# Other pacing of two lonely transforms, joint turns of two gradients in one PSUM bank, and two coefficient planes in one operation

## The chip, the core and the metric

The kernel runs on one core of a Trainium2 chip. The core has TensorE (called PE in the profile: matmuls; PEld: its weight loads), VectorE (DVE), ScalarE (ACT), GpSimd (POOL) and SyncE (SP), which here issues DMA transfers. The metric is the device time of one execution in microseconds, lower is better. Before the change the median of three runs is 1794.33 us (1794.07 to 1795.59).

## What is computed

The kernel computes a forward pass and its gradients. The input is x of shape 2048 x 576 in bf16, normalized over the last axis to xn. Two branches of xn are added to x: an S4 state space convolution (128 states for each of 576 channels, a causal convolution of length 2048 done with Fourier transforms), and a gated feed-forward layer (FFN) with a ReLU gate and 4608 hidden columns. Outputs are the result and the gradients of x, of the S4 parameters and of the three FFN weights.

```python
def _A_ref(u, A_re, A_im, B_re, B_im, C_re, C_im, log_dt, Dskip):      # S4, shortened
    dt = exp(log_dt)[:, None]
    P = exp((dt * A)[:, :, None] * l)
    K = einsum("dn,dnl,dn->dl", Cc, P, dt * Bc).real                   # the convolution's kernel
    y = irfft(rfft(pad(u)) * rfft(pad(K)))[:L]
    return y + u * Dskip
def _B_ref(x, W_gate, W_up, W_down):                                   # FFN
    gate = relu(x @ W_gate); h = gate * (x @ W_up)
    return h @ W_down
out = x + _A_ref(xn, ...) + _B_ref(xn, ...)                            # and the gradients of all inputs
```

## The kernel before

Two Python generators emit the instructions. The FFN generator is the main stream and runs over 12 chunks of 384 hidden columns. The S4 generator is woven in between: each `yield` says how many units of work were just emitted, and S4 is advanced while its sum is under 0.9 (`PACE`) of the FFN's. At the string "last", just before the final pass first needs the transforms' result, whatever is left of S4 is emitted at once.

```python
for us in ffn.gen(ln, final):
    if us == "last":
        if s4_open:
            s4_open = False
            for r in sgen:
                stt += r
        continue
    ft += us
    ...
    while s4_open and stt < PACE * (ft - start):
        r = next(sgen, None)
        ...
```

S4 works on two halves of the channels. `p1` transforms the input and the output gradient and multiplies them, `p2` builds the convolution's kernel and the parameter gradients, `p3` transforms that kernel and forms the results. `p1(0)` runs beside the parameter preparation only and `p3(1)` beside nothing else of S4; these are the lonely ones, with four buffers per pool (n = 4). The others share their time with a `p2` (n = 2). `gap` is what is yielded between the first loads of a stage and its first matmul.

```python
yield from self.both(self.p1(0, 4, 10.0), 68.0, self.params(pw), 45.0)
with ExitStack() as c:
    pools = self.p2_pools(c)
    yield from self.both(self.p2(0, pools, pw), 0.8 * W2, self.p1(1, 2, 3.0), W1)
    yield from self.both(self.p2(1, pools, pw), 0.8 * W2, self.p3(0, 2, 3.0), W3)
yield from self.p3(1, 4, 8.0)
```

A transform has three stages with results passed through DRAM: forward (`fwd1`, matmuls on L628, result A), mixing (`mix`, `product`, `unmix`: L645, L655, result C) and, in `p1`, a backward step (`back2`, L686). The last stage of `p3` is done by the final pass, which loads C.

```python
def fwd1(self, hf, ns, load, ap, op, n, gap):
    ...
    for n2 in range(ST):                         # ST = 16
        ...
            if n2 == 0:
                yield gap
        ...                                      # per ri: ns matmuls, each with one eviction
            if ri == 0:
                yield 0.2 * ns
        nc.sync.dma_start(self.A[ns][hf][:, n2], A[:])
        yield 0.2 * ns

# p1, mixing: f = 1.0 if n < 4 else 1.25; per h of 16: two mix() at f * 0.3, a product at f * 0.7,
#             an unmix() at f * 0.65; p3, mixing: f = 1.0 if n < 4 else 2.0
# p1, backward: per n2 of 16 two matmuls (L686), one eviction, yield 0.5
```

In the FFN, `a_unit` computes gate, up and the gradient of h for 128 hidden columns and 512 rows, and from them T with three parts: h, and the gradients of gate and up. Parts of earlier units are turned (transposed by TensorE, L270) between its matmul groups (L244), since the weight gradients need them the other way round; `t_steps` does that, one part per step, and `g.bal.copy` (L62 on VectorE, L68 on ScalarE) takes the result out of PSUM.

```python
self.hN = wp.tile([P, ST, Fc], BF16, name="hN")
self.dgN = wp.tile([P, ST, Fc], BF16, name="dgN")
self.duN = wp.tile([P, ST, Fc], BF16, name="duN")
...
def a_unit(self, c, sg, ft, turns=()):
    src = self.t_steps(turns)
    ...
    for i, rhs in enumerate((xT, xT, gT)):
        ...
        ps = g.psum_mm.tile([P, 512], F32, name="ps_mm")
        for k in range(NK):
            nc.tensor.matmul(ps[:], lhsT=w[:, k, fs], rhs=rhs[:, k, :], start=(k == 0), stop=(k == NK - 1))
        pss.append(ps)
        for _ in turns:
            next(src)
        yield NK * 0.2158 + len(turns) * 0.22
    ...                                          # relu (L253), mask (L254), T (L256, L261)

def t_steps(self, units):
    for c, sg, ft in units:
        for src, dst in zip(self.T[(c, sg, ft)], (self.hN, self.dgN, self.duN)):
            pt = g.psum_mm.tile([P, 512], F32, name="ps_mm")[:].bitcast(BF16).rearrange(...)
            for j in range(JS):                  # JS = 4
                nc.tensor.transpose(out=pt[:, j, :], in_=src[:, j * P:(j + 1) * P], identity=g.ident_bf[:])
            g.bal.copy(dst[:, sg * JS:(sg + 1) * JS, ft * P:(ft + 1) * P], pt[:, 0:JS, :], 512, fp32=False)
            yield
```

The pool `psum_mm` has 5 banks, the S4 pool 3. The coefficients that the last part of the change touches are applied 36 times in `p2`, on VectorE (L867 to L869):

```python
v.tensor_tensor(w1, pw[:, 2, hs]..., X[:, :, 1:3, :]..., op=ALU.mult)
v.tensor_tensor(w2, pw[:, 3, hs]..., X[:, :, 0:2, :]..., op=ALU.mult)
v.tensor_tensor(XC[:]..., w1, w2, op=ALU.subtract)
```

## Time and profile before

| | before |
|---|---|
| median of 3 runs | 1794.33 us |
| span in the profile | 1792.3 us |
| TensorE busy | 1719.7 us |
| VectorE busy | 1317.8 us |
| ScalarE busy | 1189.2 us |
| moved by DMA | 373.30 MB, mean 208 GB/s |
| turned parts taken out of PSUM | 432 copies of 128 x 512 bf16; the 412 on ScalarE have a median of 580 to 592 ns, the 20 on VectorE of 420 to 424 |

The profile is a page on one execution, with views that can be asked by stretch of time, by line or by tile. In the table of stretches each row is a stretch, in microseconds from the start: its length, the busy time of PE, PEld, DVE, ACT and POOL (in brackets the number of instructions), the clock that TensorE was granted (1.00 is full), the mean busy share of the 16 DMA engines, and GB/s. The chain of waits is the work that ended last, followed back from the end: start, length and what it was; a DMA in it is a transfer that something waited for. In the list of waits each line has the engine, what waited, and what for, with the total in us, the number of times and the longest. Busy TensorE is modelled: matmuls overlap, so small gaps between them do not show as idle.

### The profile page before, as it was taken

The numbers are of one execution on the slowest core, as the hardware profiler recorded it, in microseconds if no ns is written. First come the engines' busy times: TensorE is split into PE (matmuls) and PEld (weight loads), VectorE is DVE, ScalarE is ACT, GpSimd is POOL, SyncE is SP. The second block draws the span as 40 slices with busy tenths as digits, with TensorE's granted clock in tenths as the row PEclk, the third lists the DMA queues.
The fourth block names the chain that finished last, engine by engine and source line by source line (L and its number), as shares of the span: only waits on it lengthen the run. The fifth ranks groups of instructions, "written<-read, shape, count | busy, mean of one in ns | idle before, by whom it ended". The sixth has DMA issues, their size and how long they took to land.

```text
span 1792.3 us, 42070 instructions
## 1 busy us (share of the span) xinstructions
PE 1719.7 (96%) x16449; PEld 1184.7 (66%) x16449; DVE 1317.8 (74%) x2867; ACT 1189.2 (66%) x2736; POOL 205.0 (11%) x246
## 2 busy tenths in 40 slices
PE   7989989999999999999999999999999998999998
PEld 5665557667667666766766766766676675676776
DVE  7575884677789788678787889889978962972551
ACT  5875874786688477568468658747857845864651
POOL 0200112011022011012101101101111100110000
PEclk9999999999999999999999999999999999999999
DMA  9799989679568656766858856866766578995873
GB/s 297 265 332 303 331 233 295 194 182 253 165 145 228 192 139 157 226 183 147 229 154 190 230 156 142 212 188 151 181 185 152 112 212 257 260 288 157 270 240 100
DMA packets 239004, 373.30 MB, mean 208 GB/s; under 512 B 49491, under 2 KB 153429, under 8 KB 237269
## 3 DMA queue, kind: packets, MB, share of 16 engines
q1 hardware_dynamic: 212836, 304.09, 52.4%
q0 software_dynamic: 24384, 51.92, 18.6%
q10 hardware_dynamic: 1584, 14.60, 2.3%
q8 instruction: 129, 2.11, 0.5%
q14 instruction: 71, 0.57, 0.1%
HBM read 233.10 MB, written 137.43 MB: 207 GB/s over the span
## 4 chain that ended last, share of the span: by engine, by line
PE 63%; DVE 21%; ACT 7%; DMA 6%; issue 3%; SPq 1%; POOL 0%; ACTq 0%; DVEq 0%; POOLq 0%
PE ps_mm L298 17%; PE ps_mm L244 15%; PE ps_mm L352 11%; PE ps_mm L336 6%; PE ps_mm L270 3%; DVE V L935 2%; DVE T L261 2%; DVE Sm L936 2%; DVE V L881 1%; DVE Y L882 1%; DVE Y L880 1%; DVE rg L254 1%; PE ps_mm L370 1%; DMA gT<-in_gT_dram 1%; DVE X L861 1%
## 5 line engine op out<-in xcount | busy, mean ns | idle before, releaser
L298 PE MATMUL ps_mm<-wf,T 128*128 128x288 bf16 x3456 | 481.8, 287 | 7.4 <-DVE T L256 2.6
L298 PEld LDWEIGHTS <-T 128*128 128x128 bf16 x3456 | 324.5, 98 | 97.0 <-issue 12.9
L68 ACT CAST osx<-ps_mm 128x288 bf16<-128x288 f32 x682 | 260.5, 428 | 50.5 <-PE ps_mm L298 47.6
L311 POOL DMA_DIRECT2D acc_dram<-osx x160 | 138.8, 867 | 1027.8 <-ACT osx L68 590.7
L352 PEld LDWEIGHTS <-rows 128*128 128x128 bf16 x1536 | 146.2, 98 | 95.4 <-issue 1.6
L244 PE MATMUL ps_mm<-xT,wd_150 128*128 128x512 bf16 x720 | 181.1, 379 | 4.1 <-ACT xT L153 1.6
L270 PEld LDWEIGHTS <-T 128*128 128x128 bf16 x1728 | 127.5, 98 | 86.3 <-issue 4.7
L244 PE MATMUL ps_mm<-xT,wd_151 128*128 128x512 bf16 x720 | 180.8, 380 | 0.0
L254 DVE SCALAR_TENSOR_TENSOR rg<-rg,ps_mm 128x512 bf16<-128x512 bf16 x144 | 98.2, 682 | 108.3 <-PE ps_mm L244 68.6
L244 PE MATMUL ps_mm<-gT,wd_152 128*128 128x512 bf16 x705 | 175.9, 379 | 0.7 <-DMA gT<-in_gT_dram 0.7
L270 PE MATMUL ps_mm<-ident_bf,T 128*128 128x128 bf16 x1728 | 157.6, 220 | 4.8 <-DVE T L256 1.9
L336 PE MATMUL ps_mm<-rows,hN 128*128 128x144 bf16 x2304 | 158.9, 227 | 0.0
L336 PEld LDWEIGHTS <-hN 128*128 128x128 bf16 x2304 | 148.5, 98 | 8.0 <-issue 5.4
L68 ACT CAST obw<-ps_mm 128x384 bf16<-128x384 f32 x103 | 49.2, 478 | 144.7 <-PE ps_mm L352 112.4
L352 PE MATMUL ps_mm<-dgN,rows 128*128 128x384 bf16 x768 | 136.8, 326 | 0.5 <-DMA rows<-xs_dram_141 0.5
L352 PE MATMUL ps_mm<-duN,rows 128*128 128x384 bf16 x768 | 135.6, 326 | 0.0
L253 ACT ACTIVATE rg<-ps_mm 128x512 bf16<-128x512 f32 x144 | 86.9, 603 | 52.1 <-PE ps_mm L244 51.5
L68 ACT CAST dhb<-ps_mm 128x512 bf16<-128x512 f32 x141 | 83.8, 594 | 49.6 <-PE ps_mm L244 47.7
L261 DVE TENSOR_TENSOR T<-dhb,rg 128x1024 bf16<-128x1024 bf16 x141 | 101.0, 717 | 19.4 <-ACT dhb L68 18.7
L244 PEld LDWEIGHTS <-wd_150 128*128 128x128 bf16 x720 | 66.0, 97 | 61.5 <-issue 3.7
L244 PEld LDWEIGHTS <-wd_151 128*128 128x128 bf16 x720 | 65.4, 98 | 59.9 <-issue 3.3
L244 PEld LDWEIGHTS <-wd_152 128*128 128x128 bf16 x705 | 63.4, 98 | 58.8 <-issue 1.8
(2506 smaller groups left out, 3042.2 us busy)
## 6 DMA issues: line engine op xcount, KB each, us to landing
acc_dram<-osx POOLq DMA_DIRECT2D x176, 288.0 KB, 5.1
gT<-in_gT_dram SPq DMA_DIRECT2D x48, 640.0 KB, 6.2
xT<-xT_dram SPq DMA_DIRECT2D x44, 640.0 KB, 5.8
rows<-in_gq_dram SPq DMA_DIRECT2D x48, 576.0 KB, 4.3
wf<-in_Wf_dram ACTq DMA_DIRECT2D x11, 1296.0 KB, 8.9
ex_dram<-exs SPq DMA_DIRECT2D x36, 320.0 KB, 4.6
ex<-ex_dram SPq DMA_DIRECT2D x36, 320.0 KB, 4.5
out_dram<-obw SPq DMA_DIRECT2D x96, 96.0 KB, 2.7
```

The lines of the kernel that those rows point to most:

```text
L68: self.nc.scalar.copy(out, in_)
L244: nc.tensor.matmul(ps[:], lhsT=w[:, k, fs], rhs=rhs[:, k, :], start=(k == 0), stop=(k == NK - 1))
L253: nc.scalar.activation(rg, ps_g[:], ACT.Relu)
L254: nc.vector.scalar_tensor_tensor(upm, rg, 0.0, ps_u[:], op0=ALU.is_gt, op1=ALU.mult)
L261: nc.vector.tensor_tensor(T[:, 1:3], dhb.unsqueeze(1).to_broadcast([P, 2, JS * P]), ru[:], op=ALU.mult)
L270: nc.tensor.transpose(out=pt[:, j, :], in_=src[:, j * P:(j + 1) * P], identity=g.ident_bf[:])
L298: nc.tensor.matmul(ps[:, cs], lhsT=lt, rhs=rh, start=(i == 0), stop=(i == len(mms) - 1))
L311: nc.gpsimd.dma_start(g.acc_dram[:, t, :, :], o[:], accum_op=ALU.add)
L336: nc.tensor.matmul(ps[:, ft * 144:(ft + 1) * 144], lhsT=self.hN[:, st, ft * P:(ft + 1) * P], rhs=gq[:, st, :], start=(st == 0), stop=(st = ...
L352: nc.tensor.matmul(ps[:, :Fc], lhsT=xs[:, st, 0:P], rhs=src[:, st, :], start=(st == 0), stop=(st == ST - 1))
L935: nc.vector.tensor_tensor(pr[:, vi], X[:, dx:dx + DG, r0:r0 + 2].rearrange("p d r a -> p d (r a)").unsqueeze(2).to_broadcast(sh), psg[:, 0 ...
L936: nc.vector.tensor_reduce(out=Sm[:, :, s0 + dd:s0 + dd + DG, :].rearrange("p v d j -> p v (d j)"), in_=pr.rearrange("p v d j c -> p v (d j ...
```

## The change

Four things change. The first and the last stage of the lonely transforms yield more per piece, so that they are spread over more FFN work; the mixing of `p1(0)` yields less, the gaps are shorter, and the weights of `p1(0)` against the parameter preparation change. The parameter preparation computes its coefficient rows before its exponentials. The two gradients are turned together, eight transposes into one bank and one copy out into a common tile `gN`, and the turns are dealt out anew between the three matmul groups. The two coefficient products in `p2` become one operation with a hand-built overlapping view of X, for which the two coefficient rows swap places. The purpose of the first is to keep TensorE from waiting at the turns of stages; the others save instructions with a fixed cost.

```diff
--- before.py
+++ after.py
@@ -168,8 +168,8 @@
         self.wd = [wp.tile([P, NK, Fc], BF16, name=f"wd{i}") for i in range(3)]
         self.wf = wp.tile([P, 3, FTC, D], BF16, name="wf")
         self.hN = wp.tile([P, ST, Fc], BF16, name="hN")
-        self.dgN = wp.tile([P, ST, Fc], BF16, name="dgN")
-        self.duN = wp.tile([P, ST, Fc], BF16, name="duN")
+        self.gN = wp.tile([P, 2, ST, Fc], BF16, name="gN")
+        self.dgN, self.duN = self.gN[:, 0], self.gN[:, 1]
         g.xtp = pool("ffn_xt", 2)
         self.tp = pool("ffn_t", 2 * FTC - 1)
         self.ep = pool("ffn_e", 2)
@@ -243,9 +243,10 @@
             for k in range(NK):
                 nc.tensor.matmul(ps[:], lhsT=w[:, k, fs], rhs=rhs[:, k, :], start=(k == 0), stop=(k == NK - 1))
             pss.append(ps)
-            for _ in turns:
+            n = (2 * len(turns) * (i + 1)) // 3 - (2 * len(turns) * i) // 3
+            for _ in range(n):
                 next(src)
-            yield NK * 0.2158 + len(turns) * 0.22
+            yield NK * 0.2158 + n * 0.33
         ps_g, ps_u = pss[0:2]
         shp = [P, JS * P]
         ru = self.ep.tile([P, 2, JS * P], BF16, name="rg")
@@ -264,11 +265,17 @@
     def t_steps(self, units):
         g, nc = self.g, self.g.nc
         for c, sg, ft in units:
-            for src, dst in zip(self.T[(c, sg, ft)], (self.hN, self.dgN, self.duN)):
+            src, js, fs = self.T[(c, sg, ft)], slice(sg * JS, (sg + 1) * JS), slice(ft * P, (ft + 1) * P)
+            for which in ((0,), (1, 2)):
+                n = len(which) * JS
                 pt = g.psum_mm.tile([P, 512], F32, name="ps_mm")[:].bitcast(BF16).rearrange("p (k t) -> p k t", t=P)
-                for j in range(JS):
-                    nc.tensor.transpose(out=pt[:, j, :], in_=src[:, j * P:(j + 1) * P], identity=g.ident_bf[:])
-                g.bal.copy(dst[:, sg * JS:(sg + 1) * JS, ft * P:(ft + 1) * P], pt[:, 0:JS, :], 512, fp32=False)
+                for i, w in enumerate(which):
+                    for j in range(JS):
+                        nc.tensor.transpose(out=pt[:, i * JS + j, :], in_=src[w][:, j * P:(j + 1) * P], identity=g.ident_bf[:])
+                if n == JS:
+                    g.bal.copy(self.hN[:, js, fs], pt[:, 0:n, :], n * P, fp32=False)
+                else:
+                    g.bal.copy(self.gN[:, :, js, fs], pt[:, 0:n, :].rearrange("p (i j) t -> p i j t", i=2), n * P, fp32=False)
                 yield
 
     def outdx(self, c, sg, j, last=None, turns=()):
@@ -587,9 +594,6 @@
                 nc.sync.dma_start(self.ex_dram[:, i], ex[:])
                 bal.add(d=0.75, a=0.65)
 
-            for i in range(0, 8):
-                ex_step(i)
-                yield 1.0
             p1 = pool.tile([P, D], F32, name="p1")
             p2 = pool.tile([P, D], F32, name="p2")
             v.scalar_tensor_tensor(pw[:, 1, :], Ai, 1.0 / TWO_PI, dt[:], op0=ALU.mult, op1=ALU.mult)
@@ -597,10 +601,10 @@
                 v.tensor_tensor(p1[:], Cr, y1, op=ALU.mult)
                 v.tensor_tensor(p2[:], Ci, y2, op=ALU.mult)
                 v.tensor_tensor(p1[:], p1[:], p2[:], op=op)
-                v.tensor_tensor(pw[:, 2 + j, :], p1[:], dt[:], op=ALU.mult)
+                v.tensor_tensor(pw[:, 3 - j, :], p1[:], dt[:], op=ALU.mult)
                 bal.add(d=2.6)
                 yield 2.0
-            for i in range(8, D // SX):
+            for i in range(D // SX):
                 ex_step(i)
                 yield 1.0
 
@@ -698,7 +702,7 @@
                 nc.sync.dma_start(t[:, 0], g.xn_dram[:, 2 * m:2 * m + 2, cols])
                 nc.sync.dma_start(t[:, 1], g.g_v[:, 2 * m:2 * m + 2, cols])
                 return lambda i, n2: t[:, i, n2 % 2, :]
-            yield from self.fwd1(hf, 2, load, ap, self.pool(c, f"p1_o{hf}", 2 * n - 2 * (n < 4), "right"), n, gap)
+            yield from self.slow(1.0 if n < 4 else 1.8, self.fwd1(hf, 2, load, ap, self.pool(c, f"p1_o{hf}", 2 * n - 2 * (n < 4), "right"), n, gap))
         with ExitStack() as c:
             bp = self.pool(c, f"p1_b{hf}", n, "right")
             fp = self.pool(c, f"p1_f{hf}", n, "right")
@@ -710,7 +714,7 @@
                 return b
             bs = Ahead(load_b, ST, n)
             Z = None
-            f = 1.0 if n < 4 else 1.25
+            f = 1.0 if n < 4 else 1.1
             for h in range(ST + 1):
                 old, Z = Z, None
                 if h < ST:
@@ -749,7 +753,7 @@
                 g.bal.copy(dk[:, :, n2 % 4, :], self.back2(S3[:, n2 % 2], Ct, 0).rearrange("p (g d) -> p g d", d=SC), DH)
                 if n2 % 4 == 3:
                     nc.sync.dma_start(self.dk_dram[hf][:, n2 // 4], dk[:])
-                yield 0.5
+                yield 0.5 if n < 4 else 1
 
     def p3(self, hf, n, gap):
 
@@ -765,7 +769,7 @@
                     nc.sync.dma_start(kks[0][:], self.k_dram[hf][:, m // 2])
                 kk = kks[0]
                 return lambda i, n2: kk[:, :, n2 % 4, :]
-            yield from self.fwd1(hf, 1, load, ap, self.pool(c, f"p3_o{hf}", 2 * n - 2 * (n < 4), "right"), n, gap)
+            yield from self.slow(1.0 if n < 4 else 2, self.fwd1(hf, 1, load, ap, self.pool(c, f"p3_o{hf}", 2 * n - 2 * (n < 4), "right"), n, gap))
         with ExitStack() as c:
             bp = self.pool(c, f"p3_b{hf}", n, "right")
             fp = self.pool(c, f"p3_f{hf}", n, "right")
@@ -861,12 +865,12 @@
                 v.tensor_tensor(X[:, :, 0:2, :], Wv[:, :, :, 0:16], ex[:, :, 0:16].unsqueeze(2).to_broadcast(x2), op=ALU.mult)
                 nc.scalar.activation(X[:, :, 2, :], X[:, :, 0, :], ACT.Copy, scale=-1.0)
                 XC = xop.tile([P, SX, 2, 16], BF16, name="XC")
-                xw = [P, SX, 32]
-                w1 = xp.tile(xs, F32, name="xa")[:].rearrange("p d e -> p (d e)")[:, 0:SX * 32].rearrange("p (d e) -> p d e", e=32)
-                w2 = xp.tile([P, 2, SX, NE], F32, name="W")[:].rearrange("p r d e -> p (r d e)")[:, 0:SX * 32].rearrange("p (d e) -> p d e", e=32)
-                v.tensor_tensor(w1, pw[:, 2, hs].unsqueeze(2).to_broadcast(xw), X[:, :, 1:3, :].rearrange("p d r a -> p d (r a)"), op=ALU.mult)
-                v.tensor_tensor(w2, pw[:, 3, hs].unsqueeze(2).to_broadcast(xw), X[:, :, 0:2, :].rearrange("p d r a -> p d (r a)"), op=ALU.mult)
-                v.tensor_tensor(XC[:].rearrange("p d r a -> p d (r a)"), w1, w2, op=ALU.subtract)
+                xw = [P, 2, SX, 32]
+                w = xp.tile([P, 2, SX, NE], F32, name="W")[:].rearrange("p r d e -> p (r d e)")[:, 0:2 * SX * 32].rearrange("p (w d e) -> p w d e", w=2, e=32)
+                x = X[:, :, 0:2, :].rearrange("p d r a -> p d (r a)")
+                xv = bass.AP(x.tensor, x.offset, [x.ap[0], (16, 2)] + list(x.ap[1:]))
+                v.tensor_tensor(w, pw[:, 2:4, hs].unsqueeze(3).to_broadcast(xw), xv, op=ALU.mult)
+                v.tensor_tensor(XC[:].rearrange("p d r a -> p d (r a)"), w[:, 1], w[:, 0], op=ALU.subtract)
                 bal.add(d=6.5, a=2.5)
                 yield 6.0
                 for dd in range(x0, x0 + SX, DG):
@@ -950,7 +954,7 @@
         yield 1.0
         Br, Bi, Cr, Ci = (raw[:, i, :] for i in range(4))
         S_r, S_i, T_r, T_i = Sm[:, 0, :, 0], Sm[:, 1, :, 0], Sm[:, 0, :, 1], Sm[:, 1, :, 1]
-        pA, pB, cr, ci = (pw[:, i, hs] for i in range(4))
+        pA, pB, ci, cr = (pw[:, i, hs] for i in range(4))
         ob = lambda: yop.tile([P, DG, 2, P], BF16, name="Y")[:].rearrange("p d r q -> p (d r q)")[:, 0:DH]
 
         def out(name, x, y):
@@ -1029,12 +1033,12 @@
             iota(nc, self.ev[:, 0:16], [[1, 16]], 0, 0)
             iota(nc, self.ev[:, 16:24], [[256, 8]], 0, 0)
             iota(nc, self.ev[:, 24:40], [[16, 16]], 0, 0)
-            yield from self.both(self.p1(0, 4, 10.0), 68.0, self.params(pw), 45.0)
+            yield from self.both(self.p1(0, 4, 6), 79.04, self.params(pw), 45.0)
             with ExitStack() as c:
                 pools = self.p2_pools(c)
                 yield from self.both(self.p2(0, pools, pw), 0.8 * W2, self.p1(1, 2, 3.0), W1)
                 yield from self.both(self.p2(1, pools, pw), 0.8 * W2, self.p3(0, 2, 3.0), W3)
-            yield from self.p3(1, 4, 8.0)
+            yield from self.p3(1, 4, 6)
 
 class Final:
 
```

## The prediction

> **What bounds the kernel now.** I read the busy shares first, then the slices and the two tables of stretches, then the chain of waits, then what TensorE waits for.
>
> ```profile
> span 1792.3 us, 42070 instructions
> PE 1719.7 (96%) x16449; PEld 1184.7 (66%) x16449; DVE 1317.8 (74%) x2867; ACT 1189.2 (66%) x2736; POOL 205.0 (11%) x246
> ...
> PE 63%; DVE 21%; ACT 7%; DMA 6%; issue 3%; SPq 1%; POOL 0%; ACTq 0%; DVEq 0%; POOLq 0%
> ```
>
> TensorE is open for work that does not come in only 1792.3 - 1719.7 = 72.6 us. Of that about 17 us lie in the first 45 us and after the last matmul, which the change does not touch (45.00 - 33.41 = 11.6 at the head, 1792.3 - 1755.0 - 32.46 = 4.8 at the tail). So about 56 us of open idle time are in reach of anything. The next table, by stretch, says where they are; its columns are the busy time of each engine, the granted clock, the DMA share and GB/s.
>
> ```profile
> 90.00:140.00 50.00, 42.48 (x368) 32.21 (x367) 35.06 (x67) 35.80 (x84) 3.44 (x7) 0.90 0.94 325
> 140.00:260.00 120.00, 114.29 (x852) 66.74 (x851) 90.47 (x225) 90.09 (x221) 8.50 (x10) 1.00 0.93 296
> 260.00:290.00 30.00, 23.54 (x215) 17.57 (x213) 20.57 (x46) 14.65 (x38) 5.17 (x6) 1.00 1.02 291
> 290.00:990.00 700.00, 687.38 (x6898) 477.50 (x6896) 533.35 (x1045) 487.32 (x1107) 98.03 (x103) 1.00 0.71 188
> 990.00:1485.00 495.00, 481.70 (x4982) 338.15 (x4981) 427.55 (x910) 328.71 (x730) 62.20 (x66) 1.00 0.68 175
> 1485.00:1520.00 35.00, 29.00 (x210) 17.59 (x209) 8.24 (x16) 20.53 (x54) 1.72 (x2) 0.97 0.93 279
> 1520.00:1610.00 90.00, 88.93 (x776) 59.99 (x774) 75.25 (x234) 68.56 (x183) 12.07 (x14) 0.99 0.96 275
> ```
>
> The source tells the stages apart by their lines: the first lonely transform (`p1(0)`) sends its forward matmuls (L628) from 95 to 140 us, its mixing (L645, L655) from 160 to 254, its backward step (L686) from 264 to 284; the last one (`p3(1)`) its forward matmuls from 1493 to 1508 and its mixing from 1518 to 1619. Idle time is 7.5 us in 90:140, 5.7 in 140:260, 6.5 in 260:290, 6.0 in 1485:1520 and 1.1 in 1520:1610, 26.8 us together: almost half of the reachable idle time in 18% of the span. The long middle (290 to 1485) has 12.6 + 13.3 = 25.9 us in 1195 us. In the lonely stages the DMA share is 0.93 to 1.02, in the middle 0.7. The clock of 0.90 over 50 us is another loss.
>
> The chain shows what ends those waits:
>
> ```profile
> 125.72 7.75 DMA A_ug_179<-fA_1891
> ...
> 265.07 7.28 DMA bC_4060<-C_dk_183
> ...
> 277.60 6.14 DMA bC_4223<-C_dk_183
> ...
> 1513.38 4.71 DMA b_k<-A_k_178
> ```
>
> Each is a turn from one stage to the next: what the stage before wrote to DRAM has to land, or a load of it has to come in, and both are slow on full queues (bC takes 7.28 us, where the twice as large S_ug writes of 90 to 290 us land in 5.1 in the median). The list of TensorE's waits in the middle has no such entry; it names small ones on VectorE and ScalarE:
>
> ```profile
> PE ps_mm L298 <- DVE T L256: 2.6, 3, 1.3
> ...
> PE ps_mm L270 <- DVE T L256: 1.9, 2, 1.2
> PE ps_mm L298 <- ACT duN L68: 1.8, 4, 0.6
> ```
>
> **What the skill says.** "Perfetto Trace Analysis", section "Identifying the Most-Contended Engine", warns that matmul occupancy overstates TensorE, since matmuls are pipelined. The trace agrees: L298 shows a mean of 287 ns, but 18 of them take 2.21 us in the chain, 123 ns each. So a gap of up to 160 ns hides in "busy": from 163.16 on five groups of 8 L352 matmuls begin 1.65 to 1.8 us apart, of which 8 x 162.5 = 1.30 us are work (the rate from the 16 that take 2.60). Some loss in 140:260 is thus not in my 5.7 us. "TensorE: Matmul & The Clock Gate", section "The HAM clock gate", says that an idle window of about 3.4 us halves the clock for about as long. Here the granted clock is 0.73 in 100 to 110 us, 0.83 in 130 to 140 and 0.88 in 1510 to 1520, each the ten microseconds of a long idle gap; (1 - 0.90) x 50 = 5 us of clock are missing in 90:140 alone. "Perfetto Trace Analysis", section "Optimizing Scalar/DVE Operations", gives a fixed cost for each instruction, some 50 ns on ScalarE from PSUM and 60 on VectorE in SBUF, and says that grouping helps only a saturated engine. The trace agrees in size: two 512-column copies behind each other on ScalarE start 0.49 us apart, one of 1024 columns takes 1.01 us with the overlap still in it.
>
> **The change, part by part.**
>
> 1. Pacing of `p1(0)`. The S4 task advances while its yields are under 0.9 of those of the feed-forward task (FFN). Adding them up: forward 10 + 16 x 0.8 = 22.8 before, (6 + 12.8) x 1.8 = 33.8 after; mixing 10 + 31.2 x 1.25 = 49.0 before, 6 + 31.2 x 1.1 = 40.3 after; backward 10 + 16 x 0.5 = 18 before, 6 + 16 = 22 after. Forward gets half as much time again, backward steps come half as often, mixing is 18% denser. The work is the same, so the 64 evictions and the A writes of the forward stage, and the bC loads, meet less crowded queues. Of the 7.5 us idle and 5 us of clock in 90:140 I take 5 back; of the 6.5 in 260:290, 3. Mixing shares a DMA system that is 0.93 full and now has less time and a gap of 6 in place of 10: 2 lost. Net 6 us.
>
> 2. Pacing of `p3(1)`: forward 8 + 6.4 = 14.4 before, (6 + 6.4) x 2 = 24.8 after; mixing 8 + 73.2 before, 6 + 73.2 after. Of 6.0 us idle and about 1 of clock (0.97 of 35 us) in 1485:1520 I take 3.5 back.
>
> 3. The end of S4 moves. The two sums grow by 6.4 + 8.4 = 14.8 units, 16.4 FFN units at 0.9. Laying the two sequences of yields beside each other, S4 ends at FFN unit 1270.5 before and 1286.6 after; the final pass, which reads its result, begins at about 1294.9. In the trace the last C_ydu write is issued at 1620.0 us and the first matmul that needs it starts at 1645.8, so a unit is about 1.1 us there and the slack of 26 us shrinks to about 9. A write and the load after it took 2.7 us to the load's issue here plus some 3 us to land: it just fits. I charge 1 us.
>
> 4. Joint turns. Each of 144 FFN units drops one of three evictions: two of 512 columns become one of 1024. When ScalarE is dense that is 144 x (2 x 0.49 - 0.95) = 4 us of 1189, nothing for the bound. More matters on TensorE: transposes stay 1728, but fewer PSUM tiles are taken (5 in place of 6 per unit against 5 buffers), and with one unit to turn the first turn comes after the second matmul group, not the first, so that T has some 1.1 us longer. The waits on T, rg and the turned copies in the list sum to about 9 us. I take 2.5.
>
> 5. Coefficient planes. 36 times two VectorE multiplies of 512 fp32 columns become one of 1024: starts are 0.60 us apart, a joint one should take about 0.60 + 0.53, so 36 x 0.07 = 2.5 us of 1317.8. VectorE is nearly full only in a few stretches of the middle (43.1 of 45 us in one). I take 1.
>
> 6. The reordered parameter steps move the same work by a few units: 0.
>
> Sum: 6 + 3.5 - 1 + 2.5 + 1 = 12, so 1794.3 - 12 = 1782.
>
> **Rivals.** (a) The bandwidth rival: the lonely stages are bound by DMA, not by bursts. The share of 0.93 over 140:260 speaks for it; then the idle time moves from the turns into the denser mixing, and parts 1 and 2 give about 2 instead of 9.5 us: 1789. Against it: the open idle sits at the turns (7.5 and 6.5 us in 80 us), not inside mixing (5.7 us in 120). (b) The late end: S4's last writes queue as they did at 1588.57, where one took 13.04 us on the chain; then the final pass waits 5 to 8 us and halves its clock once: 1789 to 1792. Against it: the new end lies in 1610 to 1650, where the DMA share is 0.44 now. (c) Longer holds: a PSUM tile with two gradients is freed after one eviction of 1.0 us rather than 0.6, and L298 waits for banks: 2 to 5 us lost over 144 units. (d) The optimist: the hidden gaps inside 140:260 and the clock come back as well: 1770.
>
> **Range and chances.** The reachable loss is about 27 us open, 6 of clock and perhaps 20 hidden in the two lonely stages, and I cannot see more than half coming back, so 1768 is the lower end; with (a), (b) and (c) together the gain is gone, 1794. Two per cent is 36 us, more than all open idle time of these stages, so faster by over 2% is 0.03; slower by over 2% would need a new stall of 36 us, 0.02.
>
> **What would show it.** Right: the chain without the 7 us bC steps, no clock under 0.9 in 100 to 140, DMA share under 0.95 there; TensorE idle in 90:290 down from 19.7 to about 12; 288 turned evictions in place of 432, gN near 1.0 us; XC's multiply near 1.2 us. Wrong: more idle inside mixing (160 to 255), or a wait of L298 on bC loads at about 1635.

## The result, and the profile after

The changed kernel takes 1810.18 us (median of 4 runs, 1806.56 to 1813.08), the kernel before 1794.96 us in the same comparison (4 runs, 1794.07 to 1796.92). The ratio is 1.0082, with a 95% interval of 1.0062 to 1.0103: the change costs about 15 us, where a gain of 12 was predicted.

The first lines of the changed kernel's page, the span and the busy times:

```profile
span 1808.4 us, 41903 instructions
PE 1723.8 (95%) x16449; PEld 1188.5 (66%) x16449; DVE 1314.7 (73%) x2829; ACT 1174.5 (65%) x2594; POOL 204.0 (11%) x246
```

TensorE does the same 16449 matmuls and is open for 1808.4 - 1723.8 = 84.6 us, against 72.6 before. ScalarE and VectorE were relieved (1174.5 from 1189.2, 1314.7 from 1317.8), as intended, and the time rose all the same. The table of stretches says where (length, busy PE, PEld, DVE, ACT, POOL, granted clock, DMA share, GB/s):

```profile
90.00:140.00 50.00, 40.25 (x378) 31.86 (x377) 31.52 (x55) 32.86 (x71) 3.41 (x7) 0.90 0.87 301
140.00:260.00 120.00, 115.18 (x841) 66.62 (x839) 91.16 (x226) 91.11 (x219) 8.49 (x10) 1.00 0.95 305
260.00:290.00 30.00, 25.29 (x201) 18.03 (x198) 21.71 (x48) 15.45 (x38) 4.24 (x5) 0.89 0.89 246
290.00:990.00 700.00, 677.39 (x6765) 470.88 (x6763) 520.33 (x1008) 468.40 (x1022) 93.10 (x99) 0.99 0.70 187
990.00:1485.00 495.00, 478.92 (x5021) 339.29 (x5020) 421.58 (x876) 333.54 (x713) 67.12 (x70) 1.00 0.67 174
1485.00:1520.00 35.00, 34.98 (x263) 20.54 (x261) 20.62 (x47) 14.17 (x29) 1.34 (x2) 1.00 0.65 202
1520.00:1610.00 90.00, 84.39 (x689) 56.23 (x687) 59.84 (x173) 63.92 (x164) 12.47 (x15) 0.98 0.96 265
```

Read row by row against before. The first lonely stage did not fill up: 9.8 us are open in 90:140 (7.5 before) at the same clock of 0.90, and in 260:290 the clock fell from 1.00 to 0.89. TensorE's open time in 90:290, which should have come down from 19.7 to about 12 us, is 19.3. The largest new loss is in 290:990, with 22.6 us open, 12.6 before; 6.0 of them lie in its first 10 us, where the stretched backward step of `p1(0)` ends. At the end the 6.0 us of 1485:1520 are gone from that row, and 5.6 open us have come up in 1520:1610, where there were 1.1. The stage itself has moved there: the forward matmuls of `p3(1)` now run from 1520 to 1544 us and its mixing from 1553 on, 1493 and 1518 before.

Rows of equal times shift against each other once a kernel falls behind. I therefore aligned the two traces by the FFN's own work: every chunk has 192 matmuls of the gradient of W_down and then 128 of the gradients of gate and up, in the same order in all kernels, so the start of the n-th tells how late a kernel is. The table gives that lateness against the kernel before in us, counted from the first matmul, each number from one profiled run (single runs of one kernel differ by some us, most of it in 90 to 330, so what is read is the jump from one column to the next in a row):

| kernel | chunk 2, W_down starts (286.6 us) | chunk 2, gate and up start (302.5) | chunk 6 ends (910.1) | chunk 10 ends (1486.7) | last matmul (1787.5) |
|---|---|---|---|---|---|
| after | +0.7 | +11.1 | +8.0 | +15.8 | +15.8 |
| p1_pace_only | +0.3 | +10.3 | +8.5 | +18.4 | +17.2 |
| deep_load | -2.7 | -2.6 | +0.3 | +9.1 | +10.1 |
| back_half | -1.1 | -1.1 | -2.2 | +10.8 | +10.4 |
| delay_only | +0.9 | +0.3 | +0.9 | +10.3 | +7.2 |
| deep_rephase | -3.2 | -2.5 | +5.3 | +9.8 | +5.3 |
| early_only | +3.7 | +10.1 | +17.2 | +19.8 | +16.4 |
| reorder_only | +11.2 | +12.8 | +11.4 | +12.1 | +13.1 |
| turns_only | +5.6 | +5.6 | +5.8 | +7.0 | +6.7 |
| coef_pure | +1.1 | +2.7 | +1.0 | +7.1 | +6.0 |
| mended | -10.4 | -8.2 | -7.4 | -3.2 | -3.6 |

The changed kernel loses its time in two places: a jump of 10.4 us between the first two columns (287 to 314 in its own time), and a slow loss of 7.8 us between chunks 6 and 10, where nothing of the lonely stages runs.

The jump has a name in the chain of waits of the changed kernel, which held bC steps of 7.28 and 6.14 us before:

```profile
263.36 4.93 DMA bC_3884<-C_dk_182
...
285.32 13.46 DMA bC_4236<-C_dk_182
```

The steps meant to go away are still there, and one has doubled. What TensorE itself waited for in 225 to 325 (engine, what, for what: total us, times, longest):

```profile
PE ps_s_4300 L690 <- DMA bC_4216<-C_dk_182: 5.2, 1, 5.2
PE ps_s_3987 L690 <- DMA bC_3884<-C_dk_182: 4.7, 1, 4.7
```

and the five microseconds in which the second-last load was awaited, in the table of stretches:

```profile
290.00:295.00 5.00, 0.22 (x4) 0.04 (x1) 1.90 (x3) 0.00 (x0) 0.85 (x1) 0.94 1.07 349
295.00:300.00 5.00, 3.74 (x27) 3.13 (x28) 1.65 (x3) 1.93 (x4) 0.00 (x0) 0.50 1.04 341
```

TensorE did 0.22 us of work in 5, and then ran at half its clock; the record of the clock shows it held for 10.2 us from 294.4. "TensorE: Matmul & The Clock Gate", section "The HAM clock gate", of the Trainium skill says that an idle window of about 3.4 us halves the clock until such a window of work has passed. The trace agrees on the size of the step, and the slow stretch here lasts three such windows, of which the first two are not full of work: a second wait, of 0.8 us for the last bC, ends at 298.8. The two waits are 6.0 us, and the 8.4 us of work at half clock lost 4.2 more: 10.2 us, the whole jump.

Why the loads were slow stands in the timeline of SyncE's queue. After:

```profile
283.87 0.86 SPq L202 DMA_DIRECT2D xT<-xT_dram  x1
284.82 0.40 SPq L742 DMA_DIRECT2D bC_4216<-C_dk_182  x1
285.32 0.43 SPq L742 DMA_DIRECT2D bC_4236<-C_dk_182  x1
285.80 0.53 SPq L196 DMA_DIRECT2D gT<-in_gT_dram  x1
```

Before:

```profile
279.15 0.32 SPq L738 DMA_DIRECT2D bC_4229<-C_dk_183  x1
...
281.38 0.49 SPq L202 DMA_DIRECT2D xT<-xT_dram  x1
```

The backward step yields 1 for each of its 16 pieces in place of 0.5, 8 units more, and `p1(0)` as a whole ends 6.36 units later. Before, its last load (144 KB) was issued 2.2 us ahead of the next FFN input and landed after 5.0 us; now the last two come behind that input (640 KB), with another of 640 KB right after and 1296 KB of weights at 288.6. The list of DMA issues of the changed kernel in 255 to 300 (KB, us from issue to landing) gives 4.7 us for the last load ahead of the input, and for the two behind it:

```profile
bC_4216<-C_dk_182 SPq DMA_DIRECT2D x1, 144.0 KB, 10.5
bC_4236<-C_dk_182 SPq DMA_DIRECT2D x1, 144.0 KB, 13.5
```

**Theories.** A: the stretched backward step meets the loads of chunk 2. B: the joint turns hold banks or engines longer. C: p2 and p3 now run against another part of the FFN (later, since the yields of `p1(0)` grew by 6.36), and the position before was a good one. D: the order of the parameter steps, which I had put at 0, makes VectorE wait.

### The profile page after: what moved, and what is told of

The parts are those of the page before. It is cut to its first block, busy times and chain, and to the rows that moved or that the text cites. A ratio compares the mean times of both kernels' runs of the same rounds, so it can differ in the third digit from the quotient of the medians.

```text
span 1808.4 us, 41903 instructions
## 1 busy us (share of the span) xinstructions
PE 1723.8 (95%) x16449; PEld 1188.5 (66%) x16449; DVE 1314.7 (73%) x2829; ACT 1174.5 (65%) x2594; POOL 204.0 (11%) x246
## 4 chain that ended last, share of the span: by engine, by line
PE 67%; DVE 18%; ACT 6%; DMA 5%; issue 3%; SPq 1%; POOL 0%; DVEq 0%; ACTq 0%
PE ps_mm L305 18%; PE ps_mm L244 17%; PE ps_mm L359 11%; PE ps_mm L343 8%; PE ps_mm L274 3%; DVE V L939 2%; DVE T L262 1%; PE ps_mm L377 1%; DVE V L885 1%; DVE rg L255 1%; DMA ex_dram<-exs 1%; DVE Y L886 1%; DVE Sm L940 1%; DMA gT<-in_gT_dram 1%; DVE Y L884 1%
## 5 line engine op out<-in xcount | busy, mean ns | idle before, releaser
L305 PEld LDWEIGHTS <-T 128*128 128x128 bf16 x3456 | 323.3, 98 | 95.6 <-issue 9.8
L359 PE MATMUL ps_mm<-gN,rows 128*128 128x384 bf16 x1536 | 267.0, 326 | 0.0
L274 PEld LDWEIGHTS <-T 128*128 128x128 bf16 x1728 | 119.5, 98 | 59.2 <-issue 1.4
L68 ACT COPY gN<-ps_mm 128x1024 bf16<-128x1024 bf16 x137 | 140.4, 1025 | 8.4 <-PE ps_mm L274 8.1
L274 PE MATMUL ps_mm<-ident_bf,T 128*128 128x128 bf16 x1728 | 141.0, 220 | 0.8 <-DVE T L257 0.7
```

Source lines behind the costliest of these rows:

```text
L68: self.nc.scalar.copy(out, in_)
L274: nc.tensor.transpose(out=pt[:, i * JS + j, :], in_=src[w][:, j * P:(j + 1) * P], identity=g.ident_bf[:])
L305: nc.tensor.matmul(ps[:, cs], lhsT=lt, rhs=rh, start=(i == 0), stop=(i == len(mms) - 1))
L359: nc.tensor.matmul(ps[:, :Fc], lhsT=xs[:, st, 0:P], rhs=src[:, st, :], start=(st == 0), stop=(st == ST - 1))
```

## The experiments

"Before" in these comparisons has a median of 1794 to 1795 us; the ratios are to it. An edit "on before" starts from the kernel before, "on after" from the changed one.

### The bC loads of the backward step

`deep_load`, on after: all 16 loads are issued when the step begins.

```diff
+            cp = self.pool(c, f"p1_e{hf}", ST if n > 3 else n + 1, "right")
-                Ct = bp.tile([P, 2, 1, DH], BF16, name="bC1")
+                Ct = cp.tile([P, 2, 1, DH], BF16, name="bC1")
-            Sx, cs = Ahead(...), Ahead(load_c, ST, n + 1)
+            Sx, cs = Ahead(...), Ahead(load_c, ST, ST if n > 3 else n + 1)
```

> The changed kernel, its pacing kept, but all 16 loads of the backward step of p1(0) are issued at the start of that step (a pool of 16 buffers in place of 5). Theory A (the loss of about 11 us at chunk 2 comes from the last bC loads, which are now issued behind the xT, gT and wf loads of chunk 2): the 5.2 us wait and the clock dip at 290 to 300 us go, total 1799 to 1802. Rival B (the loss is spread, from the joint turns or the later start of p2): no more than 3 us better, 1807 to 1811. A third possibility: the burst of 16 loads only moves the wait to the first of them, 1805 to 1810.

Measured: 1808.65 us, ratio 1.0078 (1.0057 to 1.0098).

`back_half`, on after: the backward step is paced as before. This also starts p2 and p3 8 units earlier than in the changed kernel, 1.64 ahead of their place in the kernel before.

```diff
-                yield 0.5 if n < 4 else 1
+                yield 0.5
```

> The changed kernel with one number put back: the backward step of p1(0) yields 0.5 again instead of 1. Theory A: the step ends before chunk 2's loads are issued, the 8 us of waits at 290 to 299 us go, 1799 to 1803. Rival B: 1807 to 1812. If the stretch did help the first waits of this step, some of that comes back as idle time at 265 to 285.

Measured: 1807.27 us, ratio 1.0078 (1.0055 to 1.01).

Theory A holds for its place and not for the total. With early loads the jump at chunk 2 is gone (-2.7 to -2.6 in the table), as it is in `back_half` (-1.1 to -1.1), and still the totals are only 1.5 and 2.9 us lower by the medians, not clear of noise. The list of waits of `deep_load` in 260 to 330 shows part of the reason:

```profile
ACT obw L68 <- DMA out_dram<-obw: 7.8, 2, 6.5
...
PE ps_s L922 <- ACT Kst L68: 4.4, 1, 4.4
```

TensorE is no longer held at 290, but ScalarE is held at 309 for a buffer whose write to DRAM was issued late, and TensorE behind it; the row goes from -2.6 to +3.1 by the end of chunk 2 (331.1 us). The rest is the slow loss between chunks 6 and 10 (+0.3 to +9.1 here, -2.2 to +10.8 in `back_half`), which is untouched.

### Each part alone

`p1_pace_only`, on before: the pacing of `p1(0)` alone.

```diff
-            yield from self.fwd1(hf, 2, ...)
+            yield from self.slow(1.0 if n < 4 else 1.8, self.fwd1(hf, 2, ...))
-            f = 1.0 if n < 4 else 1.25
+            f = 1.0 if n < 4 else 1.1
-                yield 0.5
+                yield 0.5 if n < 4 else 1
-            yield from self.both(self.p1(0, 4, 10.0), 68.0, self.params(pw), 45.0)
+            yield from self.both(self.p1(0, 4, 6), 79.04, self.params(pw), 45.0)
```

> The kernel before with nothing but the new pacing of p1(0) (forward 1.8, mixing 1.1, backward 1, gap 6, weight 79.04). Theory A: it carries the loss, 1803 to 1809. Rival B (the turns carry it): 1788 to 1796.

Measured: 1809.36 us, ratio 1.008 (1.0065 to 1.0096). This part alone costs as much as the whole change, with the same two losses in the table.

`p3_pace_only`, on before: the pacing of `p3(1)` alone.

```diff
-            yield from self.fwd1(hf, 1, ...)
+            yield from self.slow(1.0 if n < 4 else 2, self.fwd1(hf, 1, ...))
-            yield from self.p3(1, 4, 8.0)
+            yield from self.p3(1, 4, 6)
```

> The kernel before with the pacing of p3(1) only. By the prediction 2.5 us better, 1789 to 1795: 3 to 4 us less idle at 1485 to 1520, and up to 1 us at the start of the final pass. By the change's alignment 4 us are won by chunk 11's start and lost again by its end: 1792 to 1798.

Measured: 1793.22 us, ratio 0.9994 (0.9983 to 1.0005). The stage starts later (forward matmuls from 1505 us, mixing from 1536), and its open time moves with it: gaps in TensorE's work of over 0.4 us in 1475 to 1665 sum to 6.3 us before, 6.7 here and 5.5 in the changed kernel. In the changed kernel, the list of TensorE's waits in 1485 to 1650 has the load of the stretched forward stage first and a rest of the old turn:

```profile
PE ps_s_24994 L632 <- DMA kk<-k_dram_189: 2.9, 1, 2.9
PE ps_s_25255 L649 <- DMA b_k<-A_k_177: 1.2, 1, 1.2
```

The old turn waited 4.1 us for b_k; 2.9 + 1.2 is the same sum, most of it now inside the forward stage.

`turns_only`, on before: the joint turns alone.

```diff
-            for _ in turns:
+            n = (2 * len(turns) * (i + 1)) // 3 - (2 * len(turns) * i) // 3
+            for _ in range(n):
                 next(src)
-            for src, dst in zip(self.T[(c, sg, ft)], (self.hN, self.dgN, self.duN)):
+            for which in ((0,), (1, 2)):
...
```

> The kernel before with nothing but the joint turns of the two gradients. Theory A: 1790 to 1797, as 27 us of ScalarE time is saved off the bound. Rival B (one bank held by two gradients delays TensorE): 1800 to 1808.

Measured: 1802.22 us, ratio 1.0044 (1.0029 to 1.0059).

`coef_only`, on before: the joint coefficient multiply together with the new order of the parameter steps.

```diff
-            for i in range(0, 8):
-                ex_step(i)
-                yield 1.0
...
-            for i in range(8, D // SX):
+            for i in range(D // SX):
...
-                v.tensor_tensor(w1, pw[:, 2, hs]..., X[:, :, 1:3, :]..., op=ALU.mult)
-                v.tensor_tensor(w2, pw[:, 3, hs]..., X[:, :, 0:2, :]..., op=ALU.mult)
+                v.tensor_tensor(w, pw[:, 2:4, hs]..., xv, op=ALU.mult)
```

> The kernel before with the joint coefficient multiply, the swapped rows and the reordered parameter steps only. By the prediction 1 us better: 1790 to 1796. If VectorE waits for ScalarE's negated X in front of the one multiply, which before was hidden behind nothing either: 1794 to 1800.

Measured: 1804.78 us, ratio 1.0055 (1.0039 to 1.0071). The costs of the four parts, taken from the ratios, are 14.4, -1.1, 7.9 and 9.9 us, 31 in all; the change costs 15. The costs do not add; the parts probably meet at the same waits.

### The position of the next stages

`delay_only`, on before: 6.36 units are yielded between `p1(0)` and `p2(0)`, and nothing else is changed.

```diff
             yield from self.both(self.p1(0, 4, 10.0), 68.0, self.params(pw), 45.0)
+            yield 6.36
```

> The kernel before with one bare yield of 6.36 units between p1(0) and p2(0): no work is changed, everything of S4 from p2(0) on is emitted 6.36 units later against the FFN, as in the changed kernel. Theory C (the +8 us between 910 and 1500 us, in which the changed kernel, deep_load, back_half and p1_pace_only agree and turns_only has no part, come from the phase of p2 and p3 against the FFN): 1800 to 1806, with the rise in chunks 6 to 10. Rival (the rise has another cause, in the pacing of p1(0) itself or chance): 1791 to 1798.

Measured: 1803.14 us, ratio 1.0049 (1.0037 to 1.0061). A bare delay costs 8.8 us, and in its table row it costs them where the changed kernel has its slow loss, between chunks 6 and 10 (+0.9 to +10.3).

`deep_rephase`, on `deep_load`: the delay that the yields of `p1(0)` bring is given back.

```diff
             yield from self.both(self.p1(0, 4, 6), 79.04, self.params(pw), 45.0)
+            yield -6.36
```

> deep_load with a yield of -6.36 units between p1(0) and p2(0), so that p2 and all behind it stand against the FFN as in the kernel before; the pacing of p1(0), the joint turns, the joint coefficients and the pacing of p3(1) stay. Theories A and C together: the wait on bC and the rise in chunks 6 to 10 are both gone, 1790 to 1799. Rival: 1803 to 1811 as deep_load.

Measured: 1799.47 us, ratio 1.0026 (1.0015 to 1.0036), 9 us faster than `deep_load`.

`early_only`, on before: the next stage 6.36 units earlier.

```diff
             yield from self.both(self.p1(0, 4, 10.0), 68.0, self.params(pw), 45.0)
+            yield -6.36
```

> The kernel before with the second lonely stage 6.36 units earlier, the opposite of the delay that cost 8 us. If the kernel before stands at a tuned position from which any shift costs, 1799 to 1805 us. If only a later start costs, 1788 to 1796 us.

Measured: 1806.38 us, ratio 1.0069 (1.0049 to 1.0089). A shift to the other side costs 12 us. Here TensorE meets a new wait in 280 to 330, for p2's first work on what `p1(0)` has only just written:

```profile
PE ps_s L931 <- POOL dkc L833: 3.4, 1, 3.4
```

Theory C holds for the time: the place of p2 and p3 against the FFN is worth 9 to 12 us for 6.36 units on either side. Where the time is lost it does not settle. No single wait carries the loss between chunks 6 and 10. In the list of TensorE's waits in 870 to 1500 the longest single one is 2.7 us in the changed kernel, 2.3 in `delay_only` and 1.6 before; the others, on ScalarE and VectorE, are of 1 to 2 us each or less. Nor is the loss between chunks 6 and 10 a matter of the distance alone: `back_half`, only 1.64 units ahead of the old place, loses 13.0 us there, `early_only` 2.6, and `deep_rephase`, at the old place, still 4.5, after 9.1 us within chunk 2 (-2.5 to +6.6 at 331.1 us). Which meeting of which instructions makes the old position good was not found.

### The order of the parameter steps, and the coefficient multiply

`coef_pure`, on before: the joint multiply without the new order.

```diff
-                v.tensor_tensor(w1, pw[:, 2, hs]..., X[:, :, 1:3, :]..., op=ALU.mult)
-                v.tensor_tensor(w2, pw[:, 3, hs]..., X[:, :, 0:2, :]..., op=ALU.mult)
+                v.tensor_tensor(w, pw[:, 2:4, hs]..., xv, op=ALU.mult)
```

> The kernel before with the joint coefficient multiply alone, without the reordered parameter steps. If the 10 us of coef_only come from the order (36 exs behind each other without the pause in which their 8 buffers drained): 1792 to 1798. If from the multiply: 1800 to 1808, with the loss in 250 to 1450 us.

Measured: 1798.63 us (22 runs), ratio 1.0019 (1.001 to 1.0027).

`reorder_only`, on before: the new order alone.

```diff
-            for i in range(0, 8):
-                ex_step(i)
-                yield 1.0
...
-            for i in range(8, D // SX):
+            for i in range(D // SX):
```

> The kernel before with nothing but the reordered parameter steps (coefficient rows first, then all 36 exponentials). If they carry the difference of coef_only and coef_pure: 1799 to 1804, with the loss before 180 us. If not: 1793 to 1797.

Measured: 1803.75 us, ratio 1.0059 (1.0046 to 1.0072). Moving a few small VectorE steps costs 10.6 us. In the profiled run, 10.2 of the 13.1 us at the end are there at 175 us. The timeline of VectorE in `reorder_only` (start, length, instruction, and in brackets the idle time before it and what ended it):

```profile
125.17 1.55 DVE L585 TENSOR_TENSOR exs<-pw,ev 128x640 f32<-128x640 f32 x2
134.34 0.82 DVE L585 TENSOR_TENSOR exs<-pw,ev 128x640 f32<-128x640 f32 x1 [7.63 <-DMA ex_dram<-exs]
...
135.60 0.45 DVE L62 CAST fA<-ps_s 128x288 bf16<-128x288 f32 x1
```

The multiply of an exponential waits for one of 8 buffers, that is for an earlier result to land in DRAM. The eviction of fA stands behind it in the same queue, so TensorE waits for the DRAM write too. Before, in the same view:

```profile
133.24 0.82 DVE L585 TENSOR_TENSOR exs<-pw,ev 128x640 f32<-128x640 f32 x1 [5.89 <-DMA ex_dram<-exs]
...
134.87 0.45 DVE L62 CAST fA_2069<-ps_s_2096 128x288 bf16<-128x288 f32 x1
```

The same queueing existed before, milder; there the steps on the coefficient rows stood behind the eighth exponential, which probably gave the writes time to land. What TensorE waited for in 90 to 140, `reorder_only`:

```profile
PE ps_s L625 <- DVE fA L62: 10.6, 3, 7.8
```

and before:

```profile
PE ps_s_2099 L628 <- DVE fA_2069 L62: 3.1, 1, 3.1
```

"PSUM — Partial Sum Buffer", section "Engine vs sequencer instructions", says that the queues of ScalarE, VectorE and GpSimd are strictly first in, first out. The trace agrees: 7.63 us of VectorE's wait on a DMA became 7.8 us of TensorE's. The stretch shows the cost with the clock:

```profile
90.00:140.00 50.00, 37.30 (x286) 26.84 (x285) 33.23 (x61) 30.44 (x70) 3.41 (x7) 0.81 0.87 295
```

against 42.48 busy and a clock of 0.90 before. Theory D holds.

If VectorE's queue is the way the wait reaches TensorE, another engine for that multiply might cut it. `before_gp`, `turns_gp` and `fix_gp` put it on GpSimd, on the kernel before, on `turns_only` and on `deep_rephase`.

```diff
-                v.tensor_tensor(ex[:], pw[:, 0, i * SX ...
+                nc.gpsimd.tensor_tensor(ex[:], pw[:, 0, i * SX ...
```

> The kernel before with the 36 multiplies of the parameter exponentials (exs) moved from VectorE to GpSimd; all else the same, the choice of engine for every eviction too. Theory D: between 90 and 160 us an exs multiply on VectorE waits for a free buffer, that is for the landing of an ex_dram write (5.9 us in the profile before, 8.3 in coef_only), behind it in VectorE's queue stands the eviction of an fA bank, and TensorE waits for that bank (3.1 us before, 8.5 in coef_only, 6.3 in the changed kernel). Then this is better: 1786 to 1792. Rival (the DMA queues are full and TensorE waits for them whoever holds the queue): 1793 to 1799.

Measured: 1807.97 us, ratio 1.0065 (1.0051 to 1.008).

> turns_only with the exs multiplies on GpSimd. If the 7 us of turns_only come from theory D (another eviction falls to VectorE behind a waiting exs; its wait on fA is 5.5 us against 3.1): as before_gp within 3 us, 1787 to 1795. If the joint turns cost by themselves: 7 us above before_gp, 1796 to 1802.

Measured: 1814.59 us, ratio 1.0101 (1.0085 to 1.0117).

> deep_rephase (the changed kernel with all loads of the backward step issued early and the old phase of p2) with the exs multiplies on GpSimd. By theories A, C and D together the three losses are gone: 1786 to 1794. Rival: 1797 to 1803 as deep_rephase.

Measured: 1808.52 us, ratio 1.0063 (1.0047 to 1.0079).

All three are slower than what they started from, by 7 to 12 us by the ratios. The list of waits of `before_gp` in 90 to 140 points to why: the exponential itself is on ScalarE, where it now waits for GpSimd's multiply (1299 ns in the median, 818 on VectorE), and ScalarE's queue holds up evictions in the same way.

```profile
PE ps_s L628 <- ACT fA L68: 8.1, 3, 6.6
...
ACT exs L586 <- POOL exs L585: 5.3, 7, 1.0
```

So the remedy failed, while the wait it was aimed at moved as the theory has it. More than 8 buffers, the direct remedy, were not tried.

### Why joint turns cost

`turns_two`, on `turns_only`: the pair is turned into one bank and taken out by two copies of 512.

```diff
-                    g.bal.copy(self.gN[:, :, js, fs], pt[:, 0:n, :]..., n * P, fp32=False)
+                    for i in range(2):
+                        g.bal.copy(self.gN[:, i, js, fs], pt[:, i * JS:(i + 1) * JS, :], JS * P, fp32=False)
```

> turns_only, the two gradients still turned into one bank at the same places, but taken out by two copies of 512 columns instead of one of 1024. If the long eviction holds ScalarE up in front of the lonely stage's evictions: 1792 to 1798. If the places of the turns or the shared bank cost: 1800 to 1806.

Measured: 1798.34 us, ratio 1.0024 (1.0015 to 1.0032).

`turns_slots`, on `turns_only`: joint copies, but turns after the first and second matmul group and none after the third.

```diff
-            n = (2 * len(turns) * (i + 1)) // 3 - (2 * len(turns) * i) // 3
+            n = len(turns) if i < 2 else 0
```

> turns_only with one step per unit after the first and after the second matmul group and none after the third (h after the first, both gradients after the second). If the new places cost: 1792 to 1798. If the long eviction or the shared bank: 1800 to 1806.

Measured: 1795.55 us, ratio 1.001 (0.9996 to 1.0023), no longer told apart from before. So the new places of the turns cost most of the 7.9 us, the long copy probably some of it. The loss is not paid unit by unit: in the table 5.6 of the 6.7 us of `turns_only` are there when W_down starts in chunk 2. TensorE's largest wait in 90 to 290 is that of theory D there, 7.9 us in two waits on VectorE's eviction of fA, against 4.0 in two before and none in `turns_slots`. Whether this wait carries the loss was not tested by itself. "Perfetto Trace Analysis", section "Optimizing Scalar/DVE Operations", says that where an engine is not saturated but makes bubbles elsewhere, smaller instructions may let work end sooner. `turns_two` points that way, 1.0024 against 1.0044 for the long copy, though the two intervals still overlap a little. The two joint operations in the changed kernel, in the table of groups (busy us, mean ns):

```profile
L68 ACT COPY gN<-ps_mm 128x1024 bf16<-128x1024 bf16 x137 | 140.4, 1025 | 8.4 <-PE ps_mm L274 8.1
...
L872 DVE TENSOR_TENSOR W<-pw,X 128x1024 f32<-128x1024 f32 x36 | 43.8, 1218 | 1.1 <-ACT X L866 1.1
```

1025 ns replace two copies of 599 and 607, and 1218 ns two multiplies of 681: both are as short as predicted, and neither engine's time was what counted.

### The best combination

`deep_p3`, on before: the early bC loads and the pacing of `p3(1)`.

```diff
-            Sx, cs = Ahead(...), Ahead(load_c, ST, n + 1)
+            Sx, cs = Ahead(...), Ahead(load_c, ST, ST if n > 3 else n + 1)
-            yield from self.p3(1, 4, 8.0)
+            yield from self.p3(1, 4, 6)
-            yield from self.fwd1(hf, 1, ...)
+            yield from self.slow(1.0 if n < 4 else 2, self.fwd1(hf, 1, ...))
```

> The kernel before with the 16 early bC loads and the new pacing of p3(1), nothing else of the change. If the bC waits of the backward step (7.3 and 6.1 us on the chain before) can be had without a new wait: 1785 to 1791, better than both. If the burst of loads takes it back: 1793 to 1799.

Measured: 1793.99 us, ratio 0.9999 (0.9988 to 1.0009). Nothing is won by the two together.

`mended`, on `deep_rephase`: also the old order of the parameter steps, and the turns at the places of `turns_slots`.

```diff
+            for i in range(0, 8):
+                ex_step(i)
+                yield 1.0
...
-            for i in range(D // SX):
+            for i in range(8, D // SX):
-            n = (2 * len(turns) * (i + 1)) // 3 - (2 * len(turns) * i) // 3
+            n = len(turns) if i < 2 else 0
```

> The changed kernel with every cost taken out that the single runs named: the bC loads of the backward step issued at its start, the delay between the two lonely stages given back, the parameter steps in their old order, the turns at the old places. If these four are the cause, this lands at 1790 to 1797 us, level with the kernel before or a little under. Rival, that the stretched stages themselves or the joint operations cost time wherever they stand: 1799 to 1803 us, as with the first two of the four alone.

Measured: 1795.46 us (14 runs, 1789.87 to 1806.48), ratio 1.0009 (0.9994 to 1.0024). Taking out the four named costs (late loads, delay, order, places) brings the ratio from 1.0082 to 1.0009, some 13 of the 15 us, with the stretched stages and both joint operations still in place. Two rows of its stretches, from a profiled run that was one of its faster ones:

```profile
90.00:140.00 50.00, 44.64 (x409) 33.76 (x410) 31.92 (x55) 34.92 (x79) 3.42 (x7) 0.93 0.94 341
260.00:290.00 30.00, 29.81 (x334) 25.08 (x334) 15.48 (x34) 14.54 (x34) 3.45 (x4) 0.98 1.01 326
```

In that run the open time of the first row is down to 5.4 us from 7.5. The second row is nearly full (0.2 us open, 6.5 before), but the backward step starts at 257.8 us here and 264.2 before, so part of its waits lie ahead of the row: for bC loads TensorE waits 3.3 us in one wait that ends there, 6.3 in five before. That much of what the change set out to do is there. The run leads by 10.4 us at chunk 2 and by 2.3 at chunk 3 (429.5 us): most is given back at once. Neither version beats the kernel before.

## Why the prediction was wrong

**Part 1, the pacing of `p1(0)`, is the step that failed.** The prediction took "Net 6 us" as a gain; alone, this part costs 14.4 us. Three things were wrong in its sum. First, "The work is the same, so the 64 evictions and the A writes of the forward stage, and the bC loads, meet less crowded queues": the backward step was looked at by its own rate, not by what it runs into. Its longer tail met the input and weight loads of chunk 2, and the longest bC step on the chain went from 7.28 to 13.46 us. Second, the 6.36 units that p2 and p3 start later counted only for the end of S4. As a bare delay they cost 8.8 us. Third, the evictions of the forward stage did not come free sooner. TensorE's waits for them on VectorE were 4.0 us in two before; in `p1_pace_only` the list of waits in 85 to 330 has

```profile
PE ps_s L628 <- DVE fA L62: 12.0, 3, 7.3
```

By the start of W_down in chunk 2 this was made up elsewhere (+0.3), so this wait does not carry the loss.

**Part 2, `p3(1)`:** 3.5 us were expected, 1.1 measured with an interval of -1 to +3. The wait at the turn into mixing shrank from 4.1 to 1.6 us, as intended, and waits of 1.9 and 2.1 us came up inside the stretched forward stage. As in rival (a), the idle time moved and did not go, but into the forward stage and not into the mixing.

**Part 3, the later end of S4:** 1 us was charged. The last C_ydu write of the changed kernel is issued at 1652.0 us, its chain has no wait for a C_ydu load behind it, and TensorE is fully busy from 1610 to 1690. Rival (b) did not occur. No run tried the charge by itself.

**Part 4, the joint turns:** a gain of 2.5 us was expected, a loss of 7.9 measured. The duration of the copy was right (1025 ns for "near 1.0 us"). The sign was wrong because the later place of the turns was counted as room for T, while `turns_slots` shows that the new places are the main cost, and the table that it is paid before chunk 2's W_down. Rival (c), longer holds, named the long copy; `turns_two` suggests a share for it, but 2 to 5 us spread over 144 units are not what the table shows.

**Part 5, the coefficient planes:** the multiply is 1218 ns, near the 1.2 us predicted, and saves 36 x (2 x 681 - 1218) ns = 5.2 us of busy time. Yet the kernel is 3.4 us slower with it, 1 expected the other way. In its row of the table the loss lies after chunk 6 (+1.0 to +7.1). `coef_only` and `mended`, which have the multiply too, lose 3.6 and 4.2 us there, `turns_only` and `reorder_only`, which don't, 1.2 and 0.7. A shifted meeting of instructions may again be the cause; no run isolated it.

**Part 6, the order of the parameter steps:** 0 was expected, 10.6 us measured alone. The step "move the same work by a few units" looked at the amount of work and not at which eviction stands behind a step that waits for a DMA.

The common fault is in the method: each part was given a saving from the idle time in its own stage, and none a cost for moving other work. The idle times were real, and the `mended` run shows that part of them can be removed; the net of that was still nothing.

## What to carry to other kernels

Before stretching a stage, lay its new end beside what the other stream issues there, above all its large loads: a load issued 2 us ahead of them landed in time, the same load behind one of them held TensorE for 5 us and halved its clock for 10. An instruction that waits for a DMA holds every eviction behind it in its engine's queue, so look at what stands behind it before changing the order. In a weave that was tuned by trial, test a bare delay first: if that costs as much as the change, the change is judged by its position and not by what it saves.

## What the runs showed that was not expected

- A shift of p2 and p3 by 6.36 units, later or earlier, costs 8.8 or 12 us, with no instruction changed.
- One TensorE wait of 5.2 us, with one of 0.8 close behind, was followed by half clock until 304.6 us, and the two cost 10.2 us.
- The costs of parts are not additive: 31 us alone, 15 together, and nothing measurable (1.0009) once four places are mended.
- The single runs of one kernel spread by 4 to 17 us where there were 12 or more (1796.49 to 1800.68 for `turns_two`, 1789.87 to 1806.48 for `mended`), so a difference of 0.2% took 12 to 22 runs.
